# A float32 Performer attention with an ELU MLP on one core: block transposes on 32-row strips and v as weights

## The chip, the cores and the metric

The program runs on one core of a Trainium2 chip. The metric is device time in microseconds (us) from the program's first to its last work. The kernel before takes 1087.62 us, the median of three runs (1086.78 to 1089.88).

The engines are named as the profile names them: PE is the matrix engine (TensorE), with PEld for its weight loads, DVE is the vector engine, ACT the scalar engine, POOL GpSimd, and SP issues the DMAs. SBUF is the on-chip memory with 128 partitions, PSUM the memory that PE writes; PSUM is used here in banks of 128 x 512 float32.

## The reference

```python
# q, k, v: [8, 8, 576, 64], omega: [128, 64], all float32
def phi(x):                              # x is scaled by 64 ** -0.25
    h = x @ omega.T - sum(x * x) / 2     # 128 features
    return exp(h - max(h)) / sqrt(128)
q_p, k_p = phi(q), phi(k)
kv  = einsum('bhsm,bhsd->bhmd', k_p, v)  # sums over the 576 tokens
z   = sum(k_p, axis=2)
out = (q_p @ kv) / (q_p @ z + 1e-6)      # per head
x   = out of all heads side by side      # [4608, 512]
h   = x @ w_in                           # w_in [512, 2048], float64
g   = where(h > 0, h, exp(min(h, 0)) - 1)
y   = g @ w_out                          # w_out [2048, 512], float64 -> float32
```

## The kernel before

**Attention, by pairs of heads.** 64 heads of 576 tokens are worked in 32 pairs, four to a batch element. A pair's tokens lie in nine chunks of 128: eight full ones, four of each head (chunk j belongs to head j % 2), and a ninth with the last 64 tokens of the one head on partitions 0 to 63 and of the other on 64 to 127. For each pair `pair` (L653) gives out five pieces of work:

- `load_pair` (L373): DMAs for q, k and v.
- `project` (L394), for k and for q: matmuls with omega, the squares, the maximum and the exponential. The result `h` is float32 with tokens on partitions and 9 x 128 features on the free axis. The later pairs use float32r matmuls of 256 columns (L488) into PSUM banks with the tag `pa`, of which there are three.
- `kv` (L521): the sum over tokens of k_p times v. `h` is the weight (128 tokens by 128 features) and v, with a column of ones beside it, is what moves: one matmul of 130 columns (L530) for the ninth chunk, eight of 65 (L535). The result has features on partitions: both heads' kv (`kvf`) and, from the ones, z.
- `finish` (L558): PE spreads z over all partitions (two transposes, L570); DVE multiplies and sums to get the denominators (L586) and their reciprocals (L595); POOL scales q_p with them (L596); PE transposes the nine chunks (L607) so that features come to the partitions; ACT copies them out of PSUM (`qh`); four matmuls with `kvf` as weights (L634), 64 output columns for each head, make the attention output, transposed, in two `pa` banks. From these ACT takes the rounded part `xh` and DVE the rest `xl`, straight into a ring that the MLP reads.

**The MLP** runs over 12 blocks of 384 tokens and 16 slices of 128 hidden features. To keep float32 accuracy each operand is split into a high and a low float32r part, and three products are added. A step is `layer1` (twelve matmuls of 384 columns, L764 to L766, into a bank with the tag `ph`, of which there are two; then ELU on ACT and DVE, and the split into `g`) and `layer2` (nine matmuls of 512 columns, L798 to L800, into three banks that accumulate over a segment). The first block's weights are converted from float64 on the chip in two halves; w1 in its split form goes to DRAM and is loaded again for every later step into three buffers `w1c` (L739).

**The order of the work.** Nothing runs in the order of the code. Every piece is an `op` with an engine, an estimated duration, a due time, the buffers it needs and sometimes a second engine that could do it. `Plan.order` (L141) simulates the engines with these estimates: whenever an engine is free in its model it takes the startable piece with the earliest due time. The lists that come of it are each engine's fixed order of instructions; on the chip an engine executes its own list in order and waits where something is not there. The constants `SEG`, `STEP_ATT`, `DUE_KV`, `KV2` and the like set due times; `mm`, `act`, `dve` and `pool` (L264 to L278) the estimated durations. Batch 0 comes before the MLP, batch 1 with its first segment, and batches 2 to 7 (pairs 8 to 31) are worked in among MLP steps later on. Pairs below `NEARLY` = 4 use other banks than `pa`.

Of the kernel before, what the change touches and what calls it, by code (L numbers as in the profile page):

```python
# [18 lines left out]
P = 128  # L19
B, H, S, D, M = 8, 8, 576, 64, 128  # L20
NHP = H // 2
# [23 lines left out]
SEG = [8.62, 6.25, 4.29, 5.37, 3.5, 5.81]  # L45
# [13 lines left out]
CONV1 = 13.71  # L59
CONV_STEP = -0.51  # L60
CONV2 = 0.84
# [6 lines left out]
DUE_Z = 12.0  # L68

NEARLY = 4  # L70

# [10 lines left out]
class Buf:  # L82


    def __init__(self, pool, shape, dtype, tag, name, n):
        self.args, self.key, self.n = (pool, shape, dtype, name), tag, n
        self.tile, self.left, self.slot, self.listed = None, 0, None, False
# [8 lines left out]
class Plan:  # L96
# [19 lines left out]
    def op(self, eng, ns, due, fn, reads=(), writes=(), nbytes=0, alt=None):  # L116
        n = len(self.tasks)
        engs = {eng: (ns, 0.0)}
        for e, *t in alt or ():
            engs[e] = tuple(t)  # L120
        f = fn if alt is not None else lambda e: fn()
        deps, bufs = set(), set()
        for k in reads:
            if k in self.writer:
                deps.add(self.writer[k])
            self.readers.setdefault(k, []).append(n)
        for k in writes:
            if k in self.writer:
                deps.add(self.writer[k])
            deps.update(self.readers.pop(k, ()))  # L130
            self.writer[k] = n
        for k in (*reads, *writes):
            b = k[0] if isinstance(k, tuple) else k
            if isinstance(b, Buf):
                bufs.add(b)
        deps.discard(n)
        for b in bufs:
            b.left += 1
        self.tasks.append((engs, due, f, deps, bufs, nbytes))

    def order(self):  # L141
# [51 lines left out]
        while len(done) < len(tasks):  # L193
            started = False
            for eng, q in queue.items():
# [3 lines left out]
                for n in q:  # L199
                    engs, due, _, _, bufs, _ = tasks[n]  # L200
                    if ready[n][eng] > now or (best is not None and due >= first):
                        continue
                    if len(engs) > 1 and not mine(n, eng):
                        continue
                    for b in bufs:
# [58 lines left out]
def mm(n, m=1):  # L264

    return m * (n / 2.4 + 2.5)
# [15 lines left out]
def performer_elu_kernel(  # L282
# [33 lines left out]

    kvs = [const.tile([P, P], F32, name=f"kvf{i}") for i in range(2)]

# [3 lines left out]
    part = dram.tile([3 * TB, DM], F32, name="part")  # L322
    xh = const.tile([P, NC, RING], F32R, name="xh")
# [196 lines left out]

    def kv(i, due):  # L521

        s = st[i]
# [32 lines left out]
        )  # L556

    def finish(i, due):  # L558

        s = st[i]  # L560
        h, z = s["hq"], s["z"]
# [6 lines left out]
        def spread():  # L568
            for a in range(2):
                nc.tensor.transpose(pz()[:, a * P:(a + 1) * P], z()[:, a:a + 1].to_broadcast([P, P]), ident)  # L570

        op("PE", 220, due - DUE_Z, spread, (z,), (pz,))
        qh = Buf(sb, [P, 2, S], F32, "qh", f"qh_{i}", 2)
        for g in range(3):
# [27 lines left out]
            )  # L602
            p = bank(i, "pa", f"pt_{i}_{g}")
# [20 lines left out]
            )  # L624
        kvf = kvs[i % 2]
# [12 lines left out]
        for half, (qs, n, p) in enumerate(halves):  # L638
            xs = slice(qs.start + (b % 2) * S, qs.stop + (b % 2) * S)
            key = (b % 2, hp, half)  # L640
            op(
                "ACT", act(n, True), d + 0.8 + half, lambda e, xs=xs, n=n, p=p: copy(e, xh[:, hp, xs], p()[:, 0:n]),
                (p,), (("xh", key),), alt=other("x_hi", "DVE", dve(n)),
# [6 lines left out]
                (p, ("xh", key)), (("xl", key),),  # L650
# [90 lines left out]
    def ring(blk):  # L741
# [3 lines left out]
        for b in range(2):  # L745
            for half, (s0, n) in enumerate(((0, 256), (256, S - 256))):
                if o < b * S + s0 + n and b * S + s0 < o + TB:
                    keys += [(b, hp, half) for hp in range(NHP)]
# [201 lines left out]
```

## Time and profile before

| | us |
|---|---|
| median of the runs (three, 1086.78 to 1089.88) | 1087.62 |
| span of the profiled execution, from its first to its last instruction | 1090.7 |
| PE busy, in the span | 1060.6 |
| ACT busy | 724.7 |
| DVE busy | 635.9 |
| POOL busy | 404.4 |

The profiled execution is one more execution of the same program; its own time is its span, with nothing to be added around it. Matmuls overlap in the array and the profile models their ends, so a matmul's duration is longer than the distance to the next one; what a matmul costs is read from the start of one to the start of the next. A row of the profile is a line of the kernel, an engine, an operation, what it writes and reads (`pn<-qh,kvf`), its shape, its count, and then busy time and mean duration in ns, and idle time of the engine before it. `128*64` in a matmul's row means 128 rows of the array by 64 columns.

### The profile page before, as it was taken

The page shows a single profiled execution, that of the slowest core. Times are in us where ns is not written, and L with a number is a line of the kernel's source. Part 1 is how long each engine was busy: PE and PEld are TensorE (multiplying, and loading weights), DVE is VectorE, ACT ScalarE, POOL GpSimd, SP SyncE. Part 2 cuts the span into 40 slices and gives each one's busy share as a digit, 9 for nine tenths or more (in the row PEclk, how much of TensorE's full clock was granted, in tenths as well). Part 3 has the DMA queues.
Part 4 walks back from the last instruction along what each step waited for, and adds up shares of the span by engine and source line. Part 5 has one row for each costly group of instructions (what it writes and reads, how often), then busy time and mean ns, then how long its engine had stood idle before and what let it go on. Part 6 is the DMA issues. An engine that isn't in the chain of part 4 may idle for free.

```text
span 1090.7 us, 19072 instructions
## 1 busy us (share of the span) xinstructions
PE 1060.6 (97%) x5971; PEld 936.8 (86%) x5971; DVE 635.9 (58%) x2403; ACT 724.7 (66%) x2027; POOL 404.4 (37%) x372
## 2 busy tenths in 40 slices
PE   7979888999999999999999999999999999999998
PEld 7867777889988888999888888899888888899987
DVE  6788988775776775225676666324566775322221
ACT  6878774546988986337888988326888888432222
POOL 3568746661223343222343233322233342222221
PEclk8889998999999999999999999999999999999999
DMA  7554656656663554434554645434444452343431
GB/s 213 171 181 161 208 188 240 218 186 205 207 205 130 169 170 150 165 118 157 176 155 153 193 139 170 162 119 150 162 155 167 157 164 79 117 164 119 161 121 63
DMA packets 53235, 176.90 MB, mean 162 GB/s; under 512 B 6032, under 2 KB 6224, under 8 KB 53136
## 3 DMA queue, kind: packets, MB, share of 16 engines
q1 hardware_dynamic: 53136, 175.69, 48.4%
q8 instruction: 48, 0.79, 0.3%
q14 instruction: 51, 0.42, 0.1%
HBM read 155.48 MB, written 20.19 MB: 161 GB/s over the span
## 4 chain that ended last, share of the span: by engine, by line
PE 79%; DVE 9%; ACT 6%; issue 3%; DMA 1%; POOL 1%; SPq 0%; DVEq 0%; POOLq 0%; ACTq 0%
PE ph L764 11%; PE acc L798 10%; PE acc L800 10%; PE ph L766 10%; PE acc L799 10%; PE ph L765 10%; PE pkv L535 4%; PE ppq L488 3%; PE pn L634 3%; PE pt L607 2%; PE ppk L488 2%; ACT hk L404 1%; DVE u_w L697 1%; DVE u_w L704 1%; DVE u_w L709 1%
## 5 line engine op out<-in xcount | busy, mean ns | idle before, releaser
L336 POOL TENSOR_TENSOR g<-e,g 128x384 fp32r<-128x384 f32 x182 | 189.2, 1040 | 547.7 <-DVE g L333 405.9
L764 PE MATMUL ph<-xh,w1c 128*128 128x384 f32 x768 | 267.5, 348 | 6.7 <-DVE e L777 6.2
L766 PE MATMUL ph<-xh,w1c 128*128 128x384 f32 x768 | 259.8, 338 | 0.0
L765 PE MATMUL ph<-xl,w1c 128*128 128x384 f32 x768 | 259.7, 338 | 0.0
L777 DVE SCALAR_TENSOR_TENSOR e<-e,ph 128x384 f32<-128x384 f32 x192 | 105.9, 552 | 237.2 <-ACT e L774 232.8
L798 PE MATMUL acc<-w2h,g 128*128 128x512 f32 x576 | 231.4, 402 | 0.0
L773 ACT ACTIVATE e<-ph 128x384 f32<-128x384 f32 x192 | 93.6, 488 | 206.4 <-PE ph L766 198.4
L800 PE MATMUL acc<-w2h,g 128*128 128x512 f32 x576 | 227.7, 395 | 0.0
L799 PE MATMUL acc<-w2l,g 128*128 128x512 f32 x576 | 227.4, 395 | 0.0
L764 PEld LDWEIGHTS ph<-xh,w1c 128*128 128x128 f32 x768 | 145.6, 190 | 20.1 <-DVE e L777 8.5
L765 PEld LDWEIGHTS ph<-xl,w1c 128*128 128x128 f32 x768 | 145.8, 190 | 7.2
L766 PEld LDWEIGHTS ph<-xh,w1c 128*128 128x128 f32 x768 | 145.4, 189 | 0.3 <-POOL w1c L336 0.3
L800 PEld LDWEIGHTS acc<-w2h,g 128*128 128x128 f32 x576 | 108.5, 188 | 25.5
L798 PEld LDWEIGHTS acc<-w2h,g 128*128 128x128 f32 x576 | 108.7, 189 | 15.1 <-issue 2.3
L799 PEld LDWEIGHTS acc<-w2l,g 128*128 128x128 f32 x576 | 108.8, 189 | 12.2
L336 POOL TENSOR_TENSOR hq<-hq,den 128x512 f32<-128x512 f32 (+1 forms) x96 | 90.4, 961 | 36.1 <-DVE den L595 24.6
L774 ACT ACTIVATE e<-e 128x384 f32<-128x384 f32 x192 | 100.7, 525 | 3.1
L333 DVE CAST g<-e 128x384 fp32r<-128x384 f32 x166 | 72.8, 439 | 23.5 <-PE acc L800 18.8
L586 DVE CUSTOM_DVE_ANT_0 junk<-hq,pz 128x128 f32<-128x128 f32 (+1 forms) x320 | 74.1, 279 | 16.9 <-PE pz L570 16.1
L506 DVE CUSTOM_DVE_ANT_0 hq<-ppq,p2q 128x128 f32<-128x128 f32 x216 | 54.3, 287 | 41.8 <-ACT p2q L497 40.2
L506 DVE CUSTOM_DVE_ANT_0 hk<-ppk,p2k 128x128 f32<-128x128 f32 x225 | 56.5, 286 | 36.1 <-ACT p2k L497 34.3
L497 ACT ACTIVATE p2q<-ppq,sqq 128x128 f32<-128x128 f32 x216 | 67.8, 367 | 12.5 <-PE ppq L488 10.8
(82 smaller groups left out, 1620.3 us busy)
## 6 DMA issues: line engine op xcount, KB each, us to landing
w1c<-w1s SPq DMA_DIRECT2D x176, 512.0 KB, 3.3
raw_w<-in_w_dram SPq DMA_DIRECT2D x32, 512.0 KB, 3.6
xk<-in_kx_dram SPq DMA_DIRECT2D x25, 576.0 KB, 3.9
xq<-in_qx_dram SPq DMA_DIRECT2D x24, 576.0 KB, 4.6
v<-in_v_dram SPq DMA_DIRECT2D x32, 325.0 KB, 3.4
out_dram<-o SPq DMA_DIRECT2D x36, 256.0 KB, 2.9
w1s<-w1c SPq DMA_DIRECT2D x16, 512.0 KB, 3.2
xq<-in_q_dram SPq DMA_DIRECT2D x8, 288.0 KB, 4.0
```

The costliest lines, as they stand in the source:

```text
L336: (nc.vector if e == "DVE" else nc.gpsimd).tensor_tensor(*args)
L506: nc.vector.tensor_tensor_reduce(out=h()[:, j, :], in0=view()[:, a, 0:M], in1=p2()[:, a, :], scale=1.0, scalar=LOWEST, op0=ALU.subtract, o ...
L586: nc.vector.tensor_tensor_reduce(out=junk()[r], in0=h()[r, j, :], in1=pz()[r, a * P:(a + 1) * P], scale=1.0, scalar=EPS, op0=ALU.mult, op1 ...
L764: nc.tensor.matmul(ph(), wh, xh[:, c, o:o + TB], start=(c == 0), stop=False)
L765: nc.tensor.matmul(ph(), wh, xl[:, c, o:o + TB], start=False, stop=False)
L766: nc.tensor.matmul(ph(), wl, xh[:, c, o:o + TB], start=False, stop=(c == NC - 1))
L773: op("ACT", act(TB, True), due, lambda: nc.scalar.activation(e(), ph(), AF.Relu, scale=-1.0), (p,), (e,))
L774: op("ACT", act(TB), due + 0.2, lambda: nc.scalar.activation(e(), e(), AF.Exp, scale=-1.0), (e,), (e,))
L777: lambda: nc.vector.scalar_tensor_tensor(e(), e(), -1.0, ph(), ALU.add, ALU.max), (p, e), (e,),
L798: nc.tensor.matmul(a(), g()[:, 0, ts], w2h[:, f], start=(f == f0), stop=False)
L799: nc.tensor.matmul(a(), g()[:, 0, ts], w2l[:, f], start=False, stop=False)
L800: nc.tensor.matmul(a(), g()[:, 1, ts], w2h[:, f], start=False, stop=(f == f1 - 1))
```

## The change

From pair 8 on (`NSWAP = 8`, `NTURN = 8`) three things are done in another way.

1. **The sum over keys** (`kv_swapped`): v is the weight (128 tokens by 64) and `h` moves, 128 columns a matmul; the two heads' outputs go to partitions 0 to 63 and 64 to 127 of one bank. The result has v's columns on partitions, so it is copied (`kt`), transposed by PE and copied again (`kvf`). z no longer comes out of this matmul: POOL adds the chunks of `h` over j (`zs`), ACT or DVE and POOL split the sum into two float32r parts in `zk`, and in `finish` two float32r matmuls with a matrix of ones sum them over partitions and spread them.
2. **The strips** (`replicate`): `kvf` is written to DRAM and read back by four DMAs, so that each group of 32 partitions of `zk` holds all four groups of 32 features side by side.
3. **The output** (`blocks`, `output`): DVE transposes the scaled q_p in blocks of 32 x 32 from SBUF to SBUF, in place of PE's transposes and the copies out of PSUM. After that a strip of 32 partitions e holds features for the tokens of strip e, and the output is made of 32 matmuls with 32 rows and 64 columns of weights, 160 columns each: for each of four feature groups j, four strips e and two heads a. Strip e accumulates over j in its own bank: three `pa` banks and one `ph` bank. Each bank is emptied in two instructions for `xh` and two for `xl` (128 and 32 columns).

Beside this, the order's model has other estimates (a matmul of n columns n / 2.2 + 2.5 ns, before n / 2.4 + 2.5), other due times, and a rule for tasks that need several buffers of one tag.

```diff
-SEG = [8.62, 6.25, 4.29, 5.37, 3.5, 5.81]
+SEG = [8.62, 8.43, 4.63, 5.37, 3.78, 5.1]
-PAIR0 = 9.46
-DUE_LOAD, DUE_K, DUE_KV, DUE_Q = 27.64, 24.71, 14.12, 18.02
-LOAD2, K2, KV2, Q2 = 56.0, 46.17, 30.64, 29.89
-TAIL = 11.71
+PAIR0 = 9.84
+DUE_LOAD, DUE_K, DUE_KV, DUE_Q = 34.28, 31.52, 14.12, 18.02
+LOAD2, K2, KV2, Q2 = 56.0, 46.17, 30.64, 31.34
+TAIL = 10.27
-CONV1 = 13.71
+CONV1 = 14.42
-CONV2 = 0.84
+CONV2 = 1.1
-DUE_Z = 12.0
+DUE_Z = 12.64
+NSWAP = 8
+NTURN = 8
...
                     for b in bufs:
                         if b.slot is None:
-                            s = sum(z <= now for z in slots[b.key])
-                            if s < (1 if line[b.key][-1] is b else 2 if b.key in self.LOOSE else 99):
-                                break
+                            need.setdefault(b.key, []).append(b)
+                    for key, bs in need.items():
+                        s = sum(z <= now for z in slots[key])
+                        first_in_line = all(b in bs for b in line[key][-len(bs):])
+                        if s < len(bs) + (0 if first_in_line else line[key][-1].need if key in self.LOOSE else 99):
+                            break
...
-    return m * (n / 2.4 + 2.5)
+    return m * (n / 2.2 + 2.5)
...
+    def replicate(i, due):
+        if i < NTURN:
+            return
+        s, kvf = st[i], kvs[i % 2]
+        zk = s["zk"]
+        op("SP", 500, due + 2.5, lambda: nc.sync.dma_start(kvd[i], kvf), (("kvf", i % 2),), (("kvd", i),), P * P * 4)
+        for e in range(4):
+            op(
+                "SP", 500, due + 3,
+                lambda e=e: nc.sync.dma_start(
+                    zk()[32 * e:32 * e + 32, 4 * M:].rearrange("p (j x) -> p j x", j=4), kvd[i].rearrange("(j c) x -> c j x", j=4)
+                ),
+                (("kvd", i),), ((zk, "kv", e),), P * P * 4,
+            )
+    def kv_swapped(i, due):
...
+        def mms():
+            for t in range(-1, 4):
+                for a in range(2):
+                    j, o = (8, 8 * (D + 1) + a * (D + 2)) if t < 0 else (2 * t + a, (2 * t + a) * (D + 1))
+                    nc.tensor.matmul(
+                        p()[a * D:a * D + D, 0:M], v()[:, o:o + D], h()[:, j, :], start=(t < 0), stop=(t == 3)
+                    )
+        op("PE", 5 * 216, due, mms, [*parts, v], (p,))
+        op("ACT", act(M, True), due + 1.2, lambda e: copy(e, kt(), p()[:, 0:M]), (p,), (kt,), ...)
+        op("PE", 110, due + 1.8, lambda: nc.tensor.transpose(p()[:, M:2 * M], kt(), ident), (kt,), (p,))
+        op("ACT", act(P, True), due + 2.3, lambda e: copy(e, kvf, p()[:, M:2 * M]), (p,), (("kvf", i % 2),), ...)
+        zs = Buf(sb, [P, 2, M], F32, "zs", f"zs_{i}", 1)
+        zk = s["zk"] = Buf(sb, [P, 8 * P], F32, "raw", f"zk_{i}", 3)
...
+            nc.gpsimd.tensor_tensor(zs(), h()[:, 0:2], h()[:, 2:4], ALU.add)
+            nc.gpsimd.tensor_tensor(zs(), zs(), h()[:, 4:6], ALU.add)
+            nc.gpsimd.tensor_tensor(zs(), zs(), h()[:, 6:8], ALU.add)
...
@@ finish
+                for e in range(2):
+                    nc.tensor.matmul(pz()[:, 0:2 * M], ones, zk()[:, 2 * M * e:2 * M * (e + 1)].bitcast(F32R), start=(e == 0), stop=(e == 1))
...
+    def blocks(i, g, h, qt, due):
+        n = 4 if g < 2 else 1
+        js = slice(4 * g, 4 * g + n)
+        def turn():
+            for o in range(2 if g == 2 else 1):
+                nc.vector.transpose(
+                    qt()[:, js.start + o:js.stop + o].rearrange("p j x -> p (j x)"),
+                    h()[:, js].rearrange("p j x -> p (j x)"),
+                )
+        op("DVE", (1 if g < 2 else 2) * dve(n * P), due, turn, ((h, "n", g),), ((qt, g),))
+    def output(i, qt, due):
...
+        banks = [Buf(ps, [P, 512], F32, "pa", f"pn_{i}_{e}", 3) for e in range(3)]
+        banks.append(Buf(ps, [P, 512], F32, "ph", f"pn_{i}_3", 2))
+        N = 5 * 32
+        def mms():
+            for j in range(4):
+                for e in range(4):
+                    r, c = slice(32 * e, 32 * e + 32), slice(32 * j, 32 * j + 32)
+                    for a in range(2):
+                        o = slice(a * D, a * D + D)
+                        nc.tensor.matmul(
+                            banks[e]()[o, 0:N], zk()[r, 4 * M + j * P + a * D:4 * M + j * P + a * D + D], qt()[r, a:10:2, c], start=(j == 0), stop=(j == 3)
+                        )
+        op("PE", 4 * mm(4 * N) + 200, due, mms, [*((qt, g) for g in range(3)), *((zk, "kv", e) for e in range(4))], banks)
...
```

More of the change, by code (lines that the diff above doesn't have):

```diff
@@ L86, in __init__ @@
         self.args, self.key, self.n = (pool, shape, dtype, name), tag, n
-        self.tile, self.left, self.slot, self.listed = None, 0, None, False
+        self.tile, self.left, self.slot, self.listed, self.need = None, 0, None, False, 1
     def __call__(self):
@@ L138, in op @@
             b.left += 1
+        for b in bufs:
+            if b.left == 1:
+                b.need = sum(c.key == b.key and c.left == 1 for c in bufs)
         self.tasks.append((engs, due, f, deps, bufs, nbytes))
@@ L322, in performer_elu_kernel @@
     part = dram.tile([3 * TB, DM], F32, name="part")
+    kvd = dram.tile([NPAIR, P, P], F32, name="kvd")
     xh = const.tile([P, NC, RING], F32R, name="xh")
@@ L521, in kv @@
     def kv(i, due):
+        if i >= NSWAP:
+            kv_swapped(i, due)
+            return
         s = st[i]
@@ L556, in kv @@
         )
+        replicate(i, due)
     def finish(i, due):
         s = st[i]
-        h, z = s["hq"], s["z"]
+        h = s["hq"]
+        if i >= NSWAP:
+            zk = s["zk"]
+        else:
+            z = s["z"]
         b, hp = divmod(i, NHP)
@@ L602, in finish @@
             )
+            if i >= NTURN:
+                blocks(i, g, h, qt, due - 5 + g)
+                continue
             p = bank(i, "pa", f"pt_{i}_{g}")
@@ L624, in finish @@
             )
+        if i >= NTURN:
+            output(i, qt, due - 2)
+            return
         kvf = kvs[i % 2]
@@ L639, in finish @@
             xs = slice(qs.start + (b % 2) * S, qs.stop + (b % 2) * S)
-            key = (b % 2, hp, half)
+            keys = [(b % 2, hp, half, e) for e in range(4)]
             op(
                 "ACT", act(n, True), d + 0.8 + half, lambda e, xs=xs, n=n, p=p: copy(e, xh[:, hp, xs], p()[:, 0:n]),
-                (p,), (("xh", key),), alt=other("x_hi", "DVE", dve(n)),
+                (p,), [("xh", key) for key in keys], alt=other("x_hi", "DVE", dve(n)),
             )
@@ L649, in finish @@
                 ),
-                (p, ("xh", key)), (("xl", key),),
+                (p, *(("xh", key) for key in keys)), [("xl", key) for key in keys],
+            )
+    def blocks(i, g, h, qt, due):
[6 more added lines that the diff above has]
+                    h()[:, js].rearrange("p j x -> p (j x)"),
+                )
+        op("DVE", (1 if g < 2 else 2) * dve(n * P), due, turn, ((h, "n", g),), ((qt, g),))
@@ L747, in ring @@
                 if o < b * S + s0 + n and b * S + s0 < o + TB:
-                    keys += [(b, hp, half) for hp in range(NHP)]
+                    keys += [(b, hp, half, e) for hp in range(NHP) for e in range(4)]
         return keys
```

75 lines of the change are left out of this document (73 added, 2 removed).

## The prediction

> **What bounds the kernel now.** I read the page's busy times first, then stages, then the chain of waits and the single pieces of it.
>
> ```profile
> span 1090.7 us, 19072 instructions
> PE 1060.6 (97%) x5971; PEld 936.8 (86%) x5971; DVE 635.9 (58%) x2403; ACT 724.7 (66%) x2027; POOL 404.4 (37%) x372
> PE 79%; DVE 9%; ACT 6%; issue 3%; DMA 1%; POOL 1%; SPq 0%; DVEq 0%; POOLq 0%; ACTq 0%
> ```
>
> TensorE (PE) is busy 97% of the span and makes 79% of the chain that ended last. The stages (columns: width, then busy time and instructions of PE, PEld, DVE, ACT, POOL, granted clock, DMA share, GB/s) say where it is not:
>
> ```profile
> 0.00:60.00 60.00, 51.98 (x337) 44.64 (x337) 44.06 (x158) 46.35 (x149) 29.39 (x32) 0.89 0.63 190
> 60.00:130.00 70.00, 60.96 (x374) 50.94 (x376) 62.41 (x175) 54.64 (x155) 51.67 (x41) 0.95 0.56 184
> 130.00:200.00 70.00, 62.67 (x323) 54.66 (x323) 55.47 (x115) 45.87 (x107) 39.95 (x31) 0.95 0.60 209
> 300.00:400.00 100.00, 99.73 (x597) 86.81 (x596) 70.25 (x332) 84.50 (x250) 36.07 (x35) 1.00 0.51 169
> 440.00:460.00 20.00, 20.00 (x104) 18.34 (x103) 4.57 (x10) 6.91 (x14) 5.23 (x6) 1.00 0.50 172
> ```
>
> PE idles 8.0, 9.0 and 7.3 us in the first three stages, 24.4 in all; from 300 to 400, where pairs of heads are worked in among the MLP steps, 0.3 of 100. ACT is at 84.5 and DVE at 70 there, against about a third and a quarter once no pair is under way (440 to 460). The change touches the 24 pairs from number 8 on, and these lie in the full stages: what it takes off PE's queue is time, as long as nothing else ends later.
>
> **The price of what goes.** The chain in order of time through one pair (start, duration, piece):
>
> ```profile
> 409.67 0.23 PE acc L800
> 409.89 0.22 PE pkv L530 x2
> 410.12 0.84 PE pkv L535 x8
> 410.96 0.44 PE pt L607 x4
> 411.40 0.24 PE ppq L488 x2
> 411.64 0.84 PE pkv L535 x8
> 412.48 0.44 PE pt L607 x4
> 412.92 0.17 PE ph L764
> ...
> 414.22 0.11 PE pt L607
> ...
> 416.10 0.23 PE acc L800
> 416.33 1.12 PE pn L634 x8
> 417.45 0.43 PE ppq L488 x2
> ```
>
> The pieces stand end to end, so each duration is its cost. The sums over keys (pkv): 0.22 + 0.84 + 0.84 = 1.90 us. The nine transposes (pt): 0.44 + 0.44 + 0.11 = 0.99. The outputs (pn): 1.12, and the two ppq matmuls behind them take 0.43 where two took 0.24 at 411.40: 0.19 more for leaving the half-width form, so 1.31. Together 4.20 us a pair.
>
> **The price of what comes.** A float32 matmul of the code stands in the trace as two passes (L535 has 8 a pair in the code; below there are 512 for 32 pairs):
>
> ```profile
> L535 PE MATMUL pkv<-v,hk 128*128 128x65 f32 x512 | 68.7, 280 | 0.0
> L634 PE MATMUL pn<-qh,kvf 128*64 128x320 f32 x128 | 22.7, 433 | 0.0
> ```
>
> For pn, three narrow windows of PE's timeline (from 416.27 to 416.30, from 417.02 to 417.10, and from 417.2 to 417.4):
>
> ```profile
> 416.26 0.44 PE L634 MATMUL pn<-qh,kvf 128*64 128x256 f32 x2
> 416.74 0.71 PE L634 MATMUL pn<-qh,kvf 128*64 128x320 f32 x4
> 417.01 0.44 PE L634 MATMUL pn<-qh,kvf 128*64 128x320 f32 x2
> ```
>
> Two passes start together at 416.26 and two at 417.01: the 64-column halves of the array run side by side. A slot of 320 columns lasts 416.74 to 417.01, 0.27 us, 0.84 ns a column. pn's four slots are 2 x (256 + 320) = 1152 columns, 0.97 us; the other 0.34 of its 1.31 is the price of going into and out of a split array.
>
> New kv: v is the weight, so outputs are 64 wide and two halves run as in pn. 10 matmuls, 20 passes, 10 slots of 128 columns: 1280 x 0.84 ns = 1.08, with 0.34 for the split 1.42 us; then one transpose of kt, 0.11. It is shorter than the old form since a 65-column pass there cost 0.105 us (0.84 / 8), more than its columns.
>
> New output: 32 matmuls over 32-row strips, 64 passes of 160 columns, eight tiles (four strips by two halves). If all eight run side by side: 8 slots x 160 x 0.84 ns = 1.08, plus 0.34: 1.42 us. The transposes leave PE. The spread of z, two transposes (0.22 by the 0.11 of a transpose), becomes two float32r matmuls of 256 columns (0.24 by ppq): +0.02.
>
> Sum: 4.20 - 1.42 - 0.11 - 1.42 - 0.02 = 1.23 us a pair, **29.5 us for 24 pairs**. No row shows strips side by side; that is the unknown that decides, priced below.
>
> **Beside PE.** Mean ns of one (the last number before the second bar):
>
> ```profile
> L331 ACT COPY qh<-pt 128x512 f32<-128x512 f32 x64 | 37.6, 589 | 30.5 <-PE pt L607 30.0
> L331 ACT COPY qh<-pt 128x128 f32<-128x128 f32 x32 | 8.8, 276 | 0.4 <-PE pt L607 0.4
> L331 ACT CAST xh<-pn 128x256 fp32r<-128x256 f32 x32 | 11.9, 373 | 8.0 <-PE pn L634 8.0
> L331 ACT CAST xh<-pn 128x320 fp32r<-128x320 f32 x32 | 14.1, 441 | 1.0 <-PE pn L634 1.0
> L647 DVE TENSOR_TENSOR xl<-pn,xh 128x320 fp32r<-128x320 f32 x32 | 15.5, 485 | 1.5 <-ACT xh L331 1.5
> L812 DVE TENSOR_TENSOR o<-acc,o 128x512 f32<-128x512 f32 x9 | 6.2, 690 | 2.5 <-PE acc L800 2.4
> L445 DVE TENSOR_REDUCE mxq<-ppq 128x1 f32<-128x128 f32 x8 | 2.3, 286 | 2.1 <-PE ppq L437 2.0
> L336 POOL TENSOR_TENSOR g<-e,g 128x384 fp32r<-128x384 f32 x182 | 189.2, 1040 | 547.7 <-DVE g L333 405.9
> ```
>
> ACT loses the qh copies, 2 x 0.589 + 0.276 = 1.45 us a pair. It gains the kt copy (0.28), z's cast (0.37, as xh of 256), and its two xh casts (0.81) become eight, four of 128 columns at 0.28 and four of 32, by the slope of xh (0.068 / 64 columns) about 0.21: 1.96. Net +0.35. DVE gains four block transposes: by the 512- and 128-column rows 2 x 0.69 + 2 x 0.29 = 1.96, no row shows the operation itself, and I keep half and double of that as its ends; and its two xl become eight, about +1.0: +3.0. POOL gains 1280 elements, by 1040 ns for 384 about 3.5 us a pair. The window from 300 to 440 holds eight pairs, nine pt each:
>
> ```profile
> L607 PE MATMUL pt<-ident,hq 128*128 128x128 f32 x72 | 11.4, 274 | 0.3 <-DVE mxq L506 0.3
> ```
>
> That is about six in 100 us: from 300 to 400 PE would need 92.6, ACT 86.6, DVE 88, POOL 57. All fit, with little slack left on ACT and DVE. At double price the transposes bring DVE to 100, and DVE would set the end of these stages; at half, 82. The output's first matmul waits for them and for the strips, and everything on PE stands behind it; pt waits for the same norms now and loses 0.3 us here.
>
> **The banks.** The new output takes all three pa banks and one of the two ph banks in one go; pn took two pa. No projection starts until one is free. In the trace the two banks of pn were claimed at 416.33 and given back here:
>
> ```profile
> 418.62 0.35 ACT L331 CAST xh<-pn 128x256 fp32r<-128x256 f32 x1
> 420.28 0.49 DVE L647 TENSOR_TENSOR xl<-pn,xh 128x320 fp32r<-128x320 f32 x1 [0.15 <-ACT xh L331]
> ```
>
> That is 4.4 us (to 420.77), 1.2 of it before ACT came to them. The cover is the MLP: one step is 12 x 0.17 (ph) + 9 x 0.23 (acc) = 4.1 us of PE work that needs no pa bank. With 16 emptying instructions for 4 the hold is as long or longer, and layer 1 has one ph bank meanwhile. Bounds: 0 where a step stands behind each output; else what PE loses where layer 1 waits for its bank, 6.2 us over 5 times:
>
> ```profile
> PE ph L764 <- DVE e L777: 6.2, 5, 2.9
> w1c<-w1s SPq DMA_DIRECT2D x176, 512.0 KB, 3.3
> out_dram<-o SPq DMA_DIRECT2D x36, 256.0 KB, 2.9
> SPq L739 <- PE ph L766: 420.1, 125, 7.4
> ```
>
> So 0 to 1.24 us a pair. I take **0.4**, a third, because four banks come free one after another: 24 x 0.4 = 9.6 us given back.
>
> **The added DMAs.** kvf goes out to DRAM and comes back in four strips: five issues a pair, the four behind a wait for the first's landing, some 2.9 us by out_dram. Behind them on SP's queue stand the w1c loads. SP waits for a w1c buffer up to 7.4 us because three of them run ahead; a load lands in 3.3 us and has two steps (8.2 us) from its issue to its use, so 2.9 us of delay is covered. Cost 0; without that cover it would be PE waiting up to 2.9 a pair. The strips themselves have the time from the keys' sum to the output, some 28 us by the planner's due times.
>
> **The new order.** PE's pace in the order's model becomes slower (384 columns: 162 to 177 ns; the trace has 0.17) and the due times move. What it can give is bounded by the 24.4 us of early idling; I allow 8 us either way (a third) and take 0.
>
> **The sum.** 1090.7 - 29.5 + 9.6 = 1070.8 in the profiled execution's own time. Its span lies 3.1 us above the median of the runs (1087.62), so by the runs 1087.6 - 19.9 = 1067.7; I say **1067**, and for this case alone 1052 to 1080.
>
> **Rivals.**
>
> *Strips do not run together* (ends slower). Each tile's two passes stand one behind the other in the queue, so the eighth tile's first pass has to overtake seven second passes. pn shows only one such overtaking: four passes, two halves, two starting at once. If the queue looks no further than that, two tiles run at a time: 32 slots x 0.134 + 0.34 = 4.63 us, and a pair costs 4.63 + 1.42 + 0.13 - 4.20 = 1.98 more: +47.5 us, **1135**. With four at a time 16 slots cost 2.48, the pair gains 0.17, 4 us in all, and the bank wait eats it: **1087**. The change of sign lies at 17 slots. For: no row has more than two tiles. Against: the pair of passes does overtake, and the array's halves cost no time to start together.
>
> The Trainium skill, "TensorE: Matmul & The Clock Gate", section "What overlaps and what doesn't", says that matmuls start and end strictly in program order. Under it this rival would hold (33 slots, about the same 1135); the two passes that start together at 416.26 disagree, since a half's own two passes cannot run at once.
>
> *A floor on starting passes.* If 64 short passes cannot start as fast as the slots want (one in 17 ns, 1.08 / 64), the output is paid by the pass. Nearest rows: 0.105 us a pass in pkv (then 6.7 us, +127 us: out of the question unless the halves' joint starts are an exception) and 0 between joint starts. At half as much again as the slots, 1.62, it costs 0.54 x 24 = 13: **1080**. The same page, section "Wait — 56ns, not 53.3ns?", has a floor of about 25 ns from start to start; 64 x 25 = 1.6 us would be an estimate by it of the same 1080. The joint starts go against it for two tiles; nothing here shows a long row.
>
> *Bank waits eat the gain.* At 1.24 us a pair the banks give back 29.8 us of 29.5: **1087**. For: ACT and DVE near 87 of 93 us in the pair stages. Against: PE waits 6.2 us in all for its ph bank now.
>
> **Chances.** Forecast 0.60; floor 0.07; four at a time 0.07; banks 0.09; two at a time or in order 0.17. This measurement tells about 0.3% (3.3 us) from no change: faster means under 1084.4. Faster 0.57 + 0.07 + 0.07 (half the cases at 1087, which spread some 5 us) = 0.71; same 0.09; slower 0.17 and a tail of the others, 0.20. The range reaches from full gain and 8 us of better order (1050) to the cases at 1087 with some 8 us of worse order (1095); only the case of 1135 is left out.
>
> **What would show it.** For the strips: a pair's 64 output passes in about 1.1 us of the chain, four or eight starting together; at 2.1 or 4.3 us the rival holds. For kv: 20 passes in about 1.1 us and ppq or acc behind it longer by some 0.2. For the banks: PE's waits for xl or xh in the 300 to 400 stage, about 10 us in all; ACT and DVE near 90% there. For the DMAs: no PE wait on w1c. I am wrong if the pair stages are full and PE still does not shrink, or if the gain comes from the first 200 us.

## The result and the profile after

The changed kernel takes 1106.21 us, the median of four runs (1102.89 to 1107.62), against 1087.65 for the kernel before in the same comparison (1086.78 to 1089.88): a ratio of 1.0140 with a 95% interval of 1.0119 to 1.0161. It is slower by 1.4%, and the prediction (1067 us, 1050 to 1095) missed with its range too. One execution of the kernel with the front's constants alone, further down, ran at a granted clock of 0.557 and took 1662.66 us; that kernel's figures are those of its three other runs.

The page's head after the change:

```profile
span 1105.5 us, 22389 instructions
PE 1053.6 (95%) x7171; PEld 916.0 (83%) x7171; DVE 698.7 (63%) x2644; ACT 727.2 (66%) x2144; POOL 494.7 (45%) x496
PE 64%; DVE 14%; ACT 8%; DMA 5%; POOL 4%; issue 4%; SPq 0%; POOLq 0%; DVEq 0%; ACTq 0%
```

PE is busy 7 us less than before, not 20 to 30, and idles 51.9 us of the span (1105.5 - 1053.6) where it idled 30.1. Its share of the chain that ended last falls from 79% to 64%. The stages answer where (columns as in the prediction):

```profile
0.00:60.00 60.00, 51.58 (x332) 43.84 (x333) 42.22 (x155) 43.94 (x143) 29.73 (x30) 0.89 0.60 174
60.00:130.00 70.00, 57.24 (x334) 47.57 (x333) 58.59 (x150) 49.65 (x143) 47.95 (x37) 0.88 0.51 166
130.00:200.00 70.00, 62.41 (x308) 51.74 (x308) 60.76 (x130) 41.64 (x96) 42.70 (x33) 0.93 0.62 200
300.00:400.00 100.00, 97.04 (x837) 82.01 (x837) 81.26 (x386) 83.66 (x277) 45.07 (x50) 1.00 0.55 178
```

From 60 to 130 us PE does 40 matmuls fewer than before (334 for 374), from 300 to 400 it idles 3.0 us where it idled 0.3.

How far the work has come is counted by the MLP's first layer, twelve `ph` matmuls a step. Windows of these matmuls alone (width, PE's busy time and count, granted clock, DMA share, GB/s), first before, then after:

```profile
0.00:250.00 250.00, 82.40 (x386) 0.95 0.59 198
250.00:450.00 200.00, 89.06 (x426) 1.00 0.52 171
450.00:960.00 510.00, 233.18 (x1151) 1.00 0.46 151
```

```profile
0.00:250.00 250.00, 78.39 (x348) 0.91 0.58 185
250.00:450.00 200.00, 85.82 (x409) 0.99 0.58 190
450.00:960.00 510.00, 233.94 (x1158) 1.00 0.50 162
```

By 450 us the kernel before has run 812 of them (386 + 426), the changed one 757: some four and a half steps behind. From 450 to 960 us, where 16 of the 24 new pairs lie, the two run level (1151 and 1158).

For the experiments the trace is cut at the first `ph` matmul of a step: steps 0 to 64, and steps 64 to 160, the stage with 16 new pairs (the pair stages). The times below are differences of these starts, each from one profiled execution, so ahead of step 64 a few us can be that execution's clock and not the order's (the kernel with half of the emptying, below, shows how many). Before: 383.6 and 510.4 us; after: 400.6 and 508.4. What comes ahead of step 0 (55.1 us in both) and behind step 160 (141.6 and 141.4) is the same. So the 14.8 us between the two profiled executions are +17.0 in steps 0 to 64, -2.0 in steps 64 to 160 and -0.2 behind them. Of the 17.0 steps 0 to 24 bear 16.0 (158.6 before, 174.6 after), and they end at 229.7 us. The group of the new key sums' matmuls (duration ns least, median and most, then first and last start) begins later:

```profile
L566 PE MATMUL pkv<-hk,v x480: 272/273/324, 274.8 to 938.7; 128*64 128x128 f32 x160
```

The loss is ahead of the first new matmul, and the gain that was forecast behind it is missing. Two theories follow. **O**: the new operations are worth about what the prediction says, and the new order loses it. **B**: they cost as much as they save, by waits for the four banks, the two casts a bank or the strips, and the order matters little.

### The profile page after: what moved, and what is told of

It is laid out like the page before. It is cut to its first block, busy times and chain, and to the rows that moved or that the text cites. A ratio compares the mean times of both kernels' runs of the same rounds, so it can differ in the third digit from the quotient of the medians.

```text
span 1105.5 us, 22389 instructions
## 1 busy us (share of the span) xinstructions
PE 1053.6 (95%) x7171; PEld 916.0 (83%) x7171; DVE 698.7 (63%) x2644; ACT 727.2 (66%) x2144; POOL 494.7 (45%) x496
## 4 chain that ended last, share of the span: by engine, by line
PE 64%; DVE 14%; ACT 8%; DMA 5%; POOL 4%; issue 4%; SPq 0%; POOLq 0%; DVEq 0%; ACTq 0%
PE ph L942 9%; PE ph L944 9%; PE ph L943 9%; PE acc L978 8%; PE acc L976 8%; PE acc L977 8%; PE ppk L505 2%; PE pn L788 2%; DVE junk L687 2%; PE ppq L505 2%; DMA w1c<-w1s 2%; PE pkv L566 2%; DVE tk L353 1%; DMA xk<-in_kx_dram 1%; ACT hk L421 1%
## 5 line engine op out<-in xcount | busy, mean ns | idle before, releaser
L353 POOL TENSOR_TENSOR g<-e,g 128x384 fp32r<-128x384 f32 x160 | 165.7, 1036 | 423.2 <-DVE g L350 314.3
L976 PEld LDWEIGHTS acc<-w2h,g 128*128 128x128 f32 x576 | 109.1, 189 | 18.1 <-DVE g L350 1.9
L687 DVE CUSTOM_DVE_ANT_0 junk<-hq,pz 128x128 f32<-128x128 f32 (+1 forms) x320 | 74.1, 279 | 17.2 <-PE pz L665 14.0
L523 DVE CUSTOM_DVE_ANT_0 hk<-ppk,p2k 128x128 f32<-128x128 f32 x225 | 56.7, 287 | 36.5 <-ACT p2k L514 35.6
L350 DVE CAST g<-e 128x384 fp32r<-128x384 f32 x141 | 62.5, 443 | 22.7 <-PE acc L978 19.5
L514 ACT ACTIVATE p2k<-ppk,sqk 128x128 f32<-128x128 f32 x225 | 69.4, 374 | 8.5 <-PE ppk L505 5.7
L421 ACT ACTIVATE hk<-hk,nbk 128x128 f32<-128x128 f32 x225 | 71.5, 401 | 0.5
```

The lines of the kernel that those rows point to most:

```text
L353: (nc.vector if e == "DVE" else nc.gpsimd).tensor_tensor(*args)
L421: nc.scalar.activation(h()[:, j, :], src(j), AF.Exp, bias=nb()[:, j:j + 1], scale=SCALE)
L687: nc.vector.tensor_tensor_reduce(out=junk()[r], in0=h()[r, j, :], in1=pz()[r, a * P:(a + 1) * P], scale=1.0, scalar=EPS, op0=ALU.mult, op1 ...
L976: nc.tensor.matmul(a(), g()[:, 0, ts], w2h[:, f], start=(f == f0), stop=False)
```

## The experiments

Each edit is shown against the changed kernel unless something else is named. "Old due times" are all the constants of the kernel before, "old pace" its n / 2.4. Ratios are to the kernel before with 95% intervals.

### Which half: the order or the operations

*The old operations under the new constants and pace.* The edit is against the kernel before; the last entry of `SEG` stays as it was.

```diff
-SEG = [8.62, 6.25, 4.29, 5.37, 3.5, 5.81]
+SEG = [8.62, 8.43, 4.63, 5.37, 3.78, 5.81]
...
+LOAD2, K2, KV2, Q2 = 56.0, 46.17, 30.64, 31.34
...
-    return m * (n / 2.4 + 2.5)
+    return m * (n / 2.2 + 2.5)
```

> The kernel before, with the new due times and the new matmul pace in the order's model, and none of the new operations (the last of the six SEG values stays 5.81, since the order finds no start for the old operations with 5.1). Theory O (the front is lost to the new order): the MLP's step 32 starts at about 263 us as in the changed kernel, before 250, and the time is about 1101. Rival N (the front is lost to what the new operations bring with them: DMAs, POOL sums, buffers): step 32 starts at about 250 and the time is about 1088.

*The new operations under the old due times and pace.*

```diff
-SEG = [8.62, 8.43, 4.63, 5.37, 3.78, 5.1]
+SEG = [8.62, 6.25, 4.29, 5.37, 3.5, 5.81]
...
-LOAD2, K2, KV2, Q2 = 56.0, 46.17, 30.64, 31.34
+LOAD2, K2, KV2, Q2 = 56.0, 46.17, 30.64, 29.89
...
-    return m * (n / 2.2 + 2.5)
+    return m * (n / 2.4 + 2.5)
```

> The changed kernel with all due times and the matmul pace of before. Theory O: step 32 starts at about 250 us and the time is about 1092, that is, the changed kernel's 1106 less some 14 us. Rival N: the front stays late (step 32 at about 263) and the time is about 1106. If the PE waits in the pair stages come from the new due times too and not from the banks, the whole gain appears: about 1065.

Measured: the first 1109.67 us, 1.0172 (1.0153 to 1.0190), steps 0 to 64 in 394.8 us and 64 to 160 in 519.9. The second 1081.95 us, 0.9908 (0.9882 to 0.9934), 383.7 and 495.6. The old operations lose 1.7% by the new constants alone; the new operations gain 0.9% under the old ones. B falls. O did not come true in its details. Step 32, expected at 263 us in the first kernel and at 250 in the second if the order makes the front's loss, starts at 253.5 and 256.9; and the second kernel's 1081.95 lies between the 1092 of O and the 1065 of the whole gain. The second kernel's windows of `ph`:

```profile
0.00:250.00 250.00, 78.63 (x369) 0.93 0.58 190
250.00:450.00 200.00, 87.84 (x428) 1.00 0.59 191
450.00:960.00 510.00, 237.78 (x1199) 1.00 0.52 167
```

1199 `ph` matmuls from 450 to 960 for 1151 before: four steps more in the same time. Its chain through one new pair (start, duration, piece):

```profile
528.29 1.24 PE pkv L566 x20
529.54 0.37 PE ph L942
529.91 0.18 PE ph L943
...
534.93 1.30 PE pn L788 x64
536.23 0.37 PE ph L942
536.77 0.18 PE ph L944
```

The 64 output passes stand in the chain at 1.30 us, and the `ph` matmul behind them at 0.37 for 0.17: together 1.50. The key sums stand at 1.24, with the same 0.20 behind them. That the strips run together is seen in two narrow windows of PE's timeline, at the output's begin and 0.1 us later:

```profile
534.86 0.39 PE L788 MATMUL pn<-qt,zk 32*64 32x160 f32 x8
```

```profile
534.86 0.53 PE L788 MATMUL pn<-qt,zk 32*64 32x160 f32 x16
```

Eight passes are in flight at once, and 0.1 us later sixteen.

### The parts, under the old due times and pace

*The new rule alone.* The pairs keep the old operations; what is left of the change is the rule for several buffers of a tag, the tile of ones, and one estimate of the model that the change raises for all pairs: 240 ns for the spread of z, before 220. This run does not tell the rule and that estimate apart; "rule" below means both.

```diff
-NSWAP = 8
+NSWAP = 32
-NTURN = 8
+NTURN = 32
```

> The changed file with both switches at 32: old operations, old due times and pace; what is left of the change is the order's rule for several buffers and a constant tile of ones. The three runs with the old due times and the new operations all lose 6 us between the MLP's steps 8 and 24, before any pair with new operations is finished. If the rule does that: step 24 starts at about 220 us (before 214) and the time is about 1094. If the work for the pairs from 8 on does it: step 24 at about 214 and about 1088.

*The rule and the new key sums, without strips and output* (`NSWAP` 8, `NTURN` 32).

```diff
-NTURN = 8
+NTURN = 32
```

> v as weights and the sums of z on POOL, but the old transposes on TensorE and the old output with two banks, under the due times of before. Bank theory (the waits come from an output that takes four banks): this part keeps its own gain of about 0.35 us a pair, 24 x 0.35 = 8 us: about 1079. Rival (the swapped sum with its extra copy, transpose and POOL work makes the waits): 1088 or more.

*The rule, the strips and the new output, with the old key sums* (`NSWAP` 32, `NTURN` 8; the old `kv` makes the buffer of the strips).

```diff
-NSWAP = 8
+NSWAP = 32
...
+        if i >= NTURN:
+            s["zk"] = Buf(sb, [P, 8 * P], F32, "raw", f"zk_{i}", 3)
```

> The old sum over keys, but block transposes, strips by DMA and the output on four banks, under the due times of before. Bank theory: 0.88 us a pair of TensorE time is saved, 21 us, and about 1.0 us a pair is waited, 24: about 1090. Rival (waits come from the swapped sum): about 1067.

| | median us | ratio | steps 0-64 | 64-160 |
|---|---|---|---|---|
| rule alone | 1098.45 | 1.0079 (1.0058 to 1.0100) | 386.0 | 511.4 |
| rule and key sums | 1099.51 | 1.0070 (1.0048 to 1.0092) | 390.3 | 510.2 |
| rule, strips, output | 1088.08 | 0.9971 (0.9952 to 0.9991) | 381.7 | 504.1 |
| rule and all three | 1081.95 | 0.9908 (0.9882 to 0.9934) | 383.7 | 495.6 |

The rule alone costs 0.8% with not one new operation: it changes the order that the model makes. Against the rule alone, all the operations bring 0.9908 / 1.0079 = 0.983, some 18.6 us. The strips and the output bring 1.1% of that by themselves. The key sums bring nothing by themselves (-0.1%, intervals overlapping), where 8 us were expected from the 0.35 us a pair of their prices, but 0.6% on top of the strips (0.9908 to 0.9971). A part's worth depends on the order that the model makes around it. The expectations of the two parts counted from the kernel before and left the rule out. That the strips' 1088.08 us fall on the 1090 of the bank theory is luck: the rule's 8.6 us stand in it, and none were reckoned.

### Which of the new order's constants

All of these have the new operations and the rule. *The slower pace alone, under old due times:*

```diff
-DUE_Z = 12.64
+DUE_Z = 12.0
...
-LOAD2, K2, KV2, Q2 = 56.0, 46.17, 30.64, 31.34
+LOAD2, K2, KV2, Q2 = 56.0, 46.17, 30.64, 29.89
```

(and the other constants of the front back too; n / 2.2 stays)

> New operations, due times of before, but the new matmul pace n / 2.2 in the order's model. The new order as a whole costs 24 us against the run with the old one (1082): 12.4 up to step 64, 12.6 in the pair stages behind it. If the pace makes the loss in the pair stages: steps 64 to 192 last about 650 us in place of 637, time about 1095. If not: about 1082.

*The two late due times of the new pairs alone* (`Q2` and `DUE_Z` new, all else old):

```diff
-SEG = [8.62, 8.43, 4.63, 5.37, 3.78, 5.1]
+SEG = [8.62, 6.25, 4.29, 5.37, 3.5, 5.81]
...
-    return m * (n / 2.2 + 2.5)
+    return m * (n / 2.4 + 2.5)
```

> New operations, old pace, and of the new due times only those that the late pairs know: Q2 31.34 for 29.89 and DUE_Z 12.64 for 12.0. If these make the loss in the pair stages: steps 64 to 192 last about 650 us, time about 1094. If not: about 637, time about 1082.

*The front's new constants alone* (`SEG`, `PAIR0`, `DUE_LOAD`, `DUE_K`, `TAIL`, `CONV1`, `CONV2` new; `Q2`, `DUE_Z` and the pace old):

```diff
-LOAD2, K2, KV2, Q2 = 56.0, 46.17, 30.64, 31.34
+LOAD2, K2, KV2, Q2 = 56.0, 46.17, 30.64, 29.89
-DUE_Z = 12.64
+DUE_Z = 12.0
-    return m * (n / 2.2 + 2.5)
+    return m * (n / 2.4 + 2.5)
```

> New operations, old pace, and of the new due times those of the front alone: SEG, PAIR0, DUE_LOAD, DUE_K, TAIL, CONV1, CONV2. If these make the front's loss: step 64 starts at about 455 us (with the old ones 443) and the pair stages behind stay at 637, time about 1094. If the pace makes it: step 64 at about 443 and about 1082.

*The front's new constants and the slower pace* (as the last, with n / 2.2 kept):

```diff
-LOAD2, K2, KV2, Q2 = 56.0, 46.17, 30.64, 31.34
+LOAD2, K2, KV2, Q2 = 56.0, 46.17, 30.64, 29.89
-DUE_Z = 12.64
+DUE_Z = 12.0
```

> New operations with the new due times of the front and the new pace, late due times of before. Alone, the front's due times bring step 64 from 443 to 437 us and leave the pair stages behind it at 637; alone, the pace brings step 64 to 438 and makes the pair stages 647. If the two add up: step 64 at about 431, pair stages about 647, time about 1080. If it is their combination that makes the changed kernel's front slow: step 64 at about 455, time about 1104.

*All new constants, with the old pace:*

```diff
-    return m * (n / 2.2 + 2.5)
+    return m * (n / 2.4 + 2.5)
```

> New operations, all new due times, pace of before. If the late due times cost the pair stages what they cost alone (637 to 653 us) and the front keeps its gain: step 64 at about 437, time about 1090. If pace and due times only fit each other in pairs: the pair stages at about 637 and 1075.

*`Q2` alone*, and *`DUE_Z` alone*, all else old (the edits against the kernel with old due times and pace):

```diff
-LOAD2, K2, KV2, Q2 = 56.0, 46.17, 30.64, 29.89
+LOAD2, K2, KV2, Q2 = 56.0, 46.17, 30.64, 31.34
```

> New operations, everything of before but Q2 = 31.34: the projection of q becomes due 0.7 us before the sum over keys (KV2 = 30.64), where it was due 0.75 us behind it (29.89). If this turn of two pieces makes the loss of the late due times: steps 64 to 192 last about 652 us, time about 1097. If not: about 637 and 1082.

```diff
-DUE_Z = 12.0
+DUE_Z = 12.64
```

> New operations, everything of before but DUE_Z = 12.64 for 12.0: only the two small matmuls that spread z become due 0.64 us earlier. If the loss of the late due times hangs on this: about 652 us for steps 64 to 192, time about 1097. If not: about 637 and 1082. If any small shift of a due time makes the order better or worse by many us: neither value, but away from 637 by several us.

| new constants, beside the rule and the operations | median us | ratio | steps 0-64 | 64-160 |
|---|---|---|---|---|
| none | 1081.95 | 0.9908 (0.9882 to 0.9934) | 383.7 | 495.6 |
| pace | 1088.07 | 0.9987 (0.9966 to 1.0008) | 379.3 | 505.7 |
| `Q2`, `DUE_Z` | 1098.89 | 1.0075 (1.0047 to 1.0102) | 386.2 | 511.1 |
| `Q2` | 1095.36 | 1.0040 (1.0023 to 1.0058) | 384.4 | 508.0 |
| `DUE_Z` | 1085.12 | 0.9943 (0.9913 to 0.9972) | 381.1 | 500.2 |
| front | 1073.63 | 0.9841 (0.9810 to 0.9873) | 382.9 | 495.4 |
| front, pace | 1100.34 | 1.0081 (1.0052 to 1.0110) | 397.1 | 508.0 |
| front, `Q2`, `DUE_Z` | 1089.26 | 0.9979 (0.9959 to 0.9998) | 383.1 | 509.4 |
| all (the changed kernel) | 1106.21 | 1.0140 (1.0119 to 1.0161) | 400.6 | 508.4 |

In steps 64 to 160 the pace costs 10.1 us, `Q2` 12.4, `DUE_Z` 4.6, but they don't add up: either of the first two, alone or with others, puts the stage at 505 to 511. (By its runs `DUE_Z` alone isn't clear of noise: the intervals 0.9913 to 0.9972 and 0.9882 to 0.9934 overlap.) In steps 0 to 64 none of these three, nor the front's constants, loses more than 0.7 us alone. It takes the front's constants and the pace together: 397.1 for 382.9, 14.2 of the 17 us that the changed kernel loses there. Expected was a loss by the front's constants themselves (1094) or none (1082); they gain, 1073.63, so both expectations missed. In the profiled executions 5.7 of the 6.9 us gained lie ahead of step 0, which the table leaves out (it starts at 53.8 us for 59.5). That the pace would lose mostly in the pair stages held.

### What a bad order does to the pair stages

*The changed kernel with half of the emptying.* The casts and subtractions of the 32 columns, the last 64 tokens of each head, are left out, so that part of `x` isn't written for the new pairs; the model keeps their time, so the order is the same. If the emptying of the four banks were what holds PE, the stage would shorten.

```diff
                 yield (lambda x: columns(x, e, False)), p()[:, 0:4 * 32].rearrange("p (t r) -> p t r", r=32)
-                if e < 2:
-                    yield (lambda x: x[0:D, hp, x0 + 512 + 32 * e:x0 + 544 + 32 * e]), p()[0:D, 4 * 32:N]
-                else:
-                    yield (lambda x: columns(x, e, True)), p()[D:P, 4 * 32:N]
```

> The changed kernel with its own order, but each of the four banks is emptied in one xh and one xl instruction in place of two: the copies of the last 64 tokens of each head, 32 columns a strip, are left out from pair 8 on (those columns of the ring keep older values). The estimates in the order's model stay, so the order is the same. If the hold of the four banks makes the waits of the pair stages: steps 64 to 160 fall from 508 to 500 us or less, time about 1095. If the waits come from the order of the other pieces: about 506, time about 1104.

*`Q2` to both sides, with the front's constants and the old pace.* `Q2` decides when a new pair's second projection is due; a theory was that it has to stay below `KV2` = 30.64, and 31.34 crosses it.

```diff
-LOAD2, K2, KV2, Q2 = 56.0, 46.17, 30.64, 29.89
+LOAD2, K2, KV2, Q2 = 56.0, 46.17, 30.64, 28.5
```

> As e8 (new operations, new due times of the front, everything else of before: 1074.5), with Q2 = 28.5 in place of 29.89: the projection of q due later behind the sum over keys. If it is the turn of the two pieces that costs in e11: the pair stages from step 64 to 160 stay at about 495 us and the time at about 1074. If any shift of this due time moves the order to another one of many: 500 or more, 1080 or more.

```diff
-LOAD2, K2, KV2, Q2 = 56.0, 46.17, 30.64, 29.89
+LOAD2, K2, KV2, Q2 = 56.0, 46.17, 30.64, 30.5
```

> As e8, with Q2 = 30.5: the projection of q moves 0.6 us ahead but stays due behind the sum over keys (30.64). If the turn of the two pieces is what costs: pair stages (steps 64 to 160) at about 495 us, time about 1074. If each shift costs: 500 to 508, time 1080 to 1087.

Measured: half of the emptying 1097.73 us, 1.0076 (1.0050 to 1.0101), with steps 64 to 160 in 507.1 us for 508.4. The emptying is not what holds the pair stages. The rest of this kernel's gain is no effect of the edit: its order is the changed kernel's, and it is ahead before the first new pair, with step 0 at 48.9 us for 55.1 and steps 0 to 24 in 171.7 for 174.6. The granted clock differs: 1.00 ahead of step 0 and 0.94 in steps 0 to 24, where the changed kernel's execution had 0.88 and 0.91. `Q2` 28.5: 1087.55 us, 0.9959 (0.9944 to 0.9973), stage 507.2. `Q2` 30.5: **1072.97 us, 0.9829 (0.9814 to 0.9844)**, stage 496.2. The stage takes 507.2, 495.4, 496.2 and 509.4 us for 28.5, 29.89, 30.5 and 31.34 (the last with `DUE_Z` new as well), so a value well below `KV2` (28.5) is as bad as one beyond it, and the theory of a crossing doesn't hold as the cause. The kernel with 30.5 is faster than the kernel before and the changed one; from the one with 29.89 (0.9841) its time can't be told apart.

What a bad order looks like on PE: its waits in steps 64 to 160 (engine, line, what ended the wait: us in all, times, longest), the longest rows of the changed kernel, then all of the kernel with new operations and old constants, then all before:

```profile
PE ppq L505 <- DVE mxq L523: 2.2, 5, 0.7
PE pn L788 <- DMA xk<-in_kx_dram: 1.8, 2, 0.9
PE ppq L505 <- ACT g L348: 1.8, 2, 0.9
PE pn L788 <- DMA w1c<-w1s: 1.7, 2, 0.9
PE ppq L505 <- DVE xl L819: 1.2, 2, 0.6
```

```profile
PE ppq L505 <- DVE mxq L523: 3.7, 4, 1.3
PE ppq L505 <- ACT kt L348: 0.6, 2, 0.3
PE acc L978 <- POOL g L353: 0.4, 2, 0.2
```

```profile
PE pt L607 <- ACT kvf L331: 0.8, 1, 0.8
PE pt L607 <- POOL hq L336: 0.4, 2, 0.2
```

The waits are 10.9 us in all in the changed kernel (9 rows, five shown), 4.7 under the old constants, 1.2 before. A load of k or of w1c has nothing to do with the output. One of these waits, seen in two windows of PE's timeline (from 571.35 to 571.40, and from 571.30 to 572.585):

```profile
571.32 0.36 PE L788 MATMUL pn<-qt,zk 32*64 32x160 f32 x4
```

```profile
571.32 0.50 PE L788 MATMUL pn<-qt,zk 32*64 32x160 f32 x8
572.58 0.32 PE L788 MATMUL pn<-qt,zk 32*64 32x160 f32 x1 [0.76 <-DMA w1c<-w1s]
```

Eight passes run, two for each of the four matmuls into the first two banks; then the output stands still. DVE's L523 ends its last reading of a projection's bank at 572.33, and the output goes on at 572.58. The pair's strips had landed by 553.5, so what it waited for was its third `pa` bank; the DMA's end only stood nearest. So the new output waits for three `pa` banks at one time, and how long depends on which projections the order has put just ahead of it. The listed waits are also not the whole. Counted from one start to the next, without waits, PE's pieces of steps 64 to 160 cost more in the same number (us):

| | old constants | changed kernel |
|---|---|---|
| `ph` | 203.4 | 206.7 |
| `acc` | 204.0 | 204.6 |
| `pn` | 21.9 | 24.3 |
| `ppk` | 17.2 | 18.1 |
| `ppq`, `pkv`, `pz` | 44.4 | 43.8 |
| pieces in all | 490.9 | 497.4 |
| waits, with those too short for the list | 4.7 | 11.1 |

So the 12.8 us between 495.6 and 508.4 are 6.4 of longer pieces and 6.4 of waits. Half of them fall on the output: 4.1 of the waits stand ahead of its passes or between them (none under the old constants), and its passes take 2.4 more. A clean one takes 1.07 us from its first start to its last; 3 of the 16 in these stages do so in the changed kernel, 11 under the old constants, and the others stop on the way. Why `ph` costs 3.2 more isn't settled. What makes an order good is not settled beyond this: PE's listed waits are 3.1 us with `Q2` 30.5 and 4.7 under old constants, and 10.9, 11.3 and 7.4 in the changed kernel and with `Q2` alone and at 28.5; but `DUE_Z` alone has 8.5 in a stage of 500.2, so their sum alone doesn't rank the orders.

### What a bad order does to the front

Steps 0 to 24 of the changed kernel, then of the kernel before (width, PE busy and count, granted clock, DMA share, GB/s):

```profile
55.10:229.70 174.60, 151.68 (x799) 0.91 0.58 190
```

```profile
55.10:213.60 158.50, 141.61 (x788) 0.96 0.58 198
```

PE idles 22.9 us for 16.9, 6.0 more, and the lower clock is worth at most (1 - 0.91) x 174.6 = 15.7 us for (1 - 0.96) x 158.5 = 6.3. The two together come near the 16 us lost there; part of the clock's share is that one execution's, as the half emptying showed. The longest waits for `xl`, the emptying of the early pairs' outputs, after and then before:

```profile
PE ppk L505 <- DVE xl L754: 3.6, 1, 3.6
PE pt L711 <- DVE xl L754: 3.0, 1, 3.0
```

```profile
PE pkv L530 <- DVE xl L647: 1.8, 2, 0.9
```

With the smaller ones PE waits 10.4 us for `xl` in these steps, before 2.1. Why the order leaves `xl` late there isn't settled.

In this stretch PE also runs slowly after idling. PE's timeline at 221.6 us (start, duration, line, matmul, and in brackets the idle time before it):

```profile
221.61 0.40 PE L978 MATMUL acc<-w2h,g 128*128 128x512 f32 x1
223.93 0.41 PE L942 MATMUL ph<-xh,w1c 128*128 128x384 f32 x1 [1.92 <-DMA w1c<-w1s]
224.18 0.34 PE L943 MATMUL ph<-xl,w1c 128*128 128x384 f32 x1
...
225.43 0.52 PE L944 MATMUL ph<-xh,w1c 128*128 128x384 f32 x1
225.75 0.52 PE L942 MATMUL ph<-xh,w1c 128*128 128x384 f32 x1
...
228.41 0.56 PE L977 MATMUL acc<-w2l,g 128*128 128x512 f32 x1
228.80 0.39 PE L978 MATMUL acc<-w2h,g 128*128 128x512 f32 x1
```

A wait of 1.92 us for w1c ends at 223.93. The matmuls run at their usual 0.17 us from start to start until 225.43; from there to 228.80 they need 0.32 (225.43 to 225.75), about twice as much: for 3.4 us PE works at half pace and loses another 1.7. A row of the clock by stages shows it for steps 16 to 24 (width, PE busy and count, granted clock, DMA share, GB/s), after and before:

```profile
192.30:229.70 37.40, 35.01 (x159) 0.91 0.62 208
```

```profile
182.50:213.60 31.10, 30.31 (x154) 1.00 0.62 222
```

Of the 6.3 us that this stage got longer, 1.6 are idle time (2.4 for 0.8), and the clock was 0.91 for 1.00: 0.09 x 37.4 = 3.4 us. The rest is not accounted for. The Trainium skill, "TensorE: Matmul & The Clock Gate", section "What's actually happening", has a clock that goes to one half after an idle window of about 3.4 us and comes back after a busy one. The 3.4 us of slow matmuls agree; an idle time of 1.92 us was enough for it here. So in the front a wait of some 2 us can be paid nearly twice. It isn't always: in the kernel with new operations and old constants a wait of 1.89 us ends at 347.83, and the granted clock stays at 1.00 from 340 to 355.

## Why the prediction was wrong

**The step that failed** is the one on the new order: "I allow 8 us either way (a third) and take 0". It measured +25 us (0.9908 to 1.0140: 2.3%), and some 34 with the rule, which the prediction doesn't name and so put at nothing (0.8%, 8.6 us, measured with the old operations). The 8 came from the early idling that an order could take away; nothing of it bounded what an order can lose. The bound was worked out from the side of the gain, in the front, and half of the loss (12.8 of the 25 us) is in the pair stages, which the kernel before had full: 0.3 us of idling in 100 gave no room to gain, and all the room to lose. Three separate constants (pace, `Q2`, `DUE_Z`) each lose there by themselves, 10.1, 12.4 and 4.6 us in the profiled executions. No rival was an order that loses: the 0.20 for slower stood almost whole on strips that do not run together, which they do.

**What bounds the kernel** was read rightly: the pieces of PE set the pair stages, and what the new operations took off PE was time, as long as the order fed it.

**The prices.** The sum for the operations was 1.23 us a pair with 0.4 given back for the banks, 19.9 us; measured against the rule alone 1.7%, 18.6 us. In steps 64 to 160 it is 511.4 - 495.6 = 15.8 us for 16 pairs, 0.99 a pair. From one start to the next PE's pieces fall there from 509.7 to 490.9 us, 1.17 a pair of 1.23, and its waits rise from 1.7 to 4.7, 0.19 a pair where 0.4 was allowed. Output: 1.50 us in the chain with the 0.20 behind it, for 1.42. Key sums: 1.44 for 1.42.

**"Strips do not run together" and "a floor on starting passes"** fell: eight, then sixteen passes in flight. The body of a clean output, from its first pass's start to its last one's, is 1.07 to 1.09 us, 17 ns a pass, as eight tiles at a time would have it. The Trainium skill's rule that matmuls start and end strictly in program order ("TensorE: Matmul & The Clock Gate", "What overlaps and what doesn't") does not hold for these two-pass matmuls. In order, at 33 slots, a clean output would take 32 x 0.134 = 4.3 us from its first start to its last. And at 571.32 us the output stood still for its third bank only after both passes of the four matmuls ahead had run, so each matmul's two passes stand together in the queue; yet the four first passes started side by side, ahead of the second ones.

**Beside PE** the estimates held. The new instructions of DVE and ACT in the changed kernel (busy time in all, mean ns):

```profile
L767 DVE STREAM_TRANSPOSE qt<-hq 128x512 f32<-128x512 f32 x48 | 33.5, 703 | 1.8 <-POOL hq L353 1.3
L767 DVE STREAM_TRANSPOSE qt<-hq 128x128 f32<-128x128 f32 x48 | 11.7, 282 | 0.1
L348 ACT CAST xh<-pn 128x128 fp32r<-128x128 f32 x96 | 24.2, 266 | 21.9 <-PE pn L788 21.3
L348 ACT CAST xh<-pn 64x32 fp32r<-64x32 f32 x96 | 17.5, 182 | 0.6
```

The block transposes are 2 x 0.703 + 2 x 0.282 = 1.97 us a pair for 1.96, `xh` 4 x 0.266 + 4 x 0.182 = 1.79 for 1.96. DVE stands at 81 from 300 to 400 where 88 was expected, ACT at 84 for 87, POOL at 45 for 57; but five new outputs lie in that stretch, where about six pairs were reckoned.

**The banks as a rival** ("the banks give back 29.8 us of 29.5") came true in size, but only under the new order: of 1.23 us a pair the changed kernel keeps 0.1 (508.4 for 510.4 before, over 16 pairs). That is luck: it isn't by the mechanism named, the emptying after the output (507.1 with half of it). The other way round, the output waits for banks that projections still hold, and its share is about half of the loss.

**The DMAs** at 0 held in the pair stages: the load of a strip lands in 2.7 us, and under the good orders PE waits there at most 0.4 us for the write of `kvf` and for no w1c. In the front the changed kernel waits 1.9 us once for a w1c, which the kernel before doesn't.

**"I am wrong if the pair stages are full and PE still does not shrink"** was the first sign: PE busy 97.0 of 100 us, and 508.4 for 510.4 in steps 64 to 160.

## What to carry to other kernels

When a change brings new operations and a newly searched order, price them apart: run the old operations under the new order, and the new operations under the old one. An order that a model lists by due times has no price that can be read off the old profile; here single constants moved the time by up to 1.3% and one step (`Q2` 29.89 to 30.5) not measurably, and the pair stages of the new operations lay anywhere between 495 and 511 us. So the spread of its neighbours is a better measure of an unknown order than the idling of the old one, and the loss is open where the stage is full. And a due time searched in a model is worth a run of its neighbours on the chip: with one number changed from a searched set (`Q2` 31.34 to 30.5) and two put back, the same operations took 1072.97 us instead of 1106.21 (0.9829 and 1.0140 of the kernel before).

## What the runs showed of the hardware

Float32 matmuls of 32 rows by 64 columns, two passes each, run eight tiles at a time in one queue: 64 passes of 160 columns in 1.07 to 1.09 us, one started each 17 ns. PE's clock fell to one half for 3.4 us after an idle time of 1.92 us, which then cost 1.7 us more, but not after one of 1.89 us elsewhere. And one and the same order reached step 0 at 48.9 us with a granted clock of 1.00 in one execution, and at 55.1 us with 0.88 in another.
